# Gated linear attention with a low-rank mixer: turned keys packed in 96 rows, one group's logarithms summed on TensorE, signs from bits, and a rearranged written order

## The chip, the cores and the metric

The kernel runs on one core of a Trainium2 chip. The metric is device time in microseconds, the median of the runs shown. Inputs and outputs are float32 in HBM; the two channel weights and the mixing weights arrive as float64 words and are turned into float32 on the chip.

## The reference

```
B, H, S, D = 4, 8, 768, 48
mag = sqrt(a_re*a_re + a_im*a_im)
scale = minimum(mag, 0.999) / (mag + 1e-06)
a_re_n, a_im_n = a_re*scale, a_im*scale
for t in range(S):
    S_re, S_im = a_re_n*S_re - a_im_n*S_im + outer(k[t], v[t]), a_re_n*S_im + a_im_n*S_re
    y[t] = q[t] @ S_re
x = y with heads side by side            # (4, 768, 384)
u = x + ((x.T @ U) @ V).T                # over the 768 tokens, rank 32
out = u + relu(u @ w_ch1) @ w_ch2        # 384 -> 1536 -> 384
```

The complex gates turn and shrink a 48 x 48 state at each token, in each of 32 heads. The kernel takes the logarithm of the shrinking and the angle of the turning, sums both along the tokens, and works on blocks of 128 tokens with matmuls.

## The kernel before, in words

The tokens of the four sequences form 24 chunks of 128. Two chunks are one group: there are 12 groups, and 12 calls of the mixer, one for each two chunks.

`gates(g)` works on the gates of a group. `magnitudes_of` (line 637) squares the inputs on ScalarE, and takes logarithms and exponentials on ScalarE and VectorE; the log of the gate's size, `l`, is the sum of a limited logarithm and a second logarithm `y` (line 659 for the first group, 663 for the others). For groups 3 and up, `l` is split into two parts of type fp32r. `within` and its `summed` (688) multiply those logs with the constant matrices `mid` and `fore` on TensorE, which sums them along the tokens; ScalarE's exponentials of that are `es` and `ef`, the weights of q and k. `of_blocks` (725) sums them over blocks of tokens, which gives the table `E`, and four DMAs on SyncE's queue copy it to `T`, one for the real, one for the imaginary half, for two sets of heads. `turns_of` (754) takes the arctangent, multiplies it by the sign of `a_re` (array `n`) and makes fractions of a turn of it; `angles` (770) sums those along the tokens on TensorE (`ph`), with an addition of 0.25 a token, and takes the fraction; `waves` makes cosine and sine, `cs`. For groups 0 to 2 (`BITS`) the sign comes from the sign bit, on VectorE (line 678); for the others ScalarE has a Sign pass (682) and an affine pass that divides by pi and adds 0.25 (583).

`prep(i)` (837) works on a chunk: VectorE multiplies q and k by `es`, then by cosine and sine, into `QKC` of 128 x 8 heads x 2 x 64, of which 48 of each 64 columns hold data and the others zeros. TensorE transposes each head's 112 columns (line 860; real part in rows 0 to 47, imaginary part in rows 64 to 111), and ScalarE copies that to `QK` (871). `chain(i)` (882) makes the products of q and k level by level: `inner` (907, 910) and `corners` (971) on TensorE, scalings by `T` on VectorE (387, in `scaled`), copies into `DG` and `AT`, then the state update `dk` (996) and the outputs `y` (1027, 1035). `mixer(m)` (1051) does the mixing and the channel matmuls of two chunks: `up` (1122), `few` (1222, a scheme with fewer products, from mixer 7 on), `down` (1313, 1356). `leave` (1292) writes the output, at the end of the last mixer on SyncE's queue.

The order of the work is written out. Each operation is recorded by `plan.add` with an engine, a planner's cost and a rank; `ORDER` (line 30) gives for each engine, kind and chunk the place of every operation in one order over all engines, 0 to 2670. The kernel emits the operations in that order, so each engine's queue is a subsequence of it, and an engine executes its queue in order. Waits follow from the data. SyncE's queue issues the input loads, the copies of `E` to `T` and of `DG` to `AT`; GpSimd's queue issues the carries of the angle sum from chunk to chunk (line 779) and most outputs.

`SPARE` (line 176) lists places before which TensorE gets filler: `idle(k)` (1507) multiplies the identity with itself into a PSUM tile that is about to be used, k pieces of 128 columns at once and at most `AHEAD` = 3, if such a tile is free:

```
        nc.tensor.matmul(out=to[:, 0:k * 128].rearrange("p (k m) -> p k m", k=k), lhsT=ident,
                         rhs=ident.unsqueeze(1).to_broadcast([128, k, 128]), start=True, stop=True)
```

The functions that the diff touches:

Of the kernel before, what the change touches and what calls it, by code (L numbers as in the profile page):

```python
# [39 lines left out]
        ("POOL", "load"): {0: [14], 1: [34], 1.5: [84], 2: [31]},  # L40
        ("DVE", "load"): {1: [58]},
# [6 lines left out]
        ("ACT", "gates"): {0: [1, 2, 4, 6, 7, 16, 17, 22, 23, 29, 28, 45, 70, 71], 1: [24, 27, 38, 39, 41, 42, 46, 47, 65, 64, 67, 68], 2: [129, 108,  # L48
# [10 lines left out]
        ("DVE", "gates"): {0: [5, 8, 13, 18, 19, 54, 49], 1: [30, 21, 40, 43, 44, 51, 50], 2: [111, 143, 156, 185, 169], 4: [277, 322, 323, 372, 356],  # L59
# [109 lines left out]
        ("POOL", "small"): {0: [932, 933], 1: [1119, 1116, 1117], 2: [1337, 1278, 1338], 3: [1670, 1446, 1515], 4: [1778, 1776, 1777], 5: [2049, 1855,  # L169
        2008], 6: [2154, 2101, 2162], 7: [2343, 2276, 2342], 8: [2633, 2632, 2648], 9: [2629, 2634, 2663], 10: [2635, 2627, 2636]},  # L170
        ("POOL", "angles"): {6: [615], 8: [708, 733], 10: [882, 931], 12: [1097], 14: [1273, 1302], 16: [1472, 1516], 18: [1669], 20: [1879, 1913],
        22: [2039, 2077]},
        ("DVE", "mixing"): {7: [2018, 2019, 2021, 2030, 2032, 2024, 2040, 2102, 2108, 2115, 2120, 2125, 2027]},
}

# [1413 lines left out]
```

## Time and profile before

| | |
|---|---|
| median of 3 runs | 628.38 us (627.25 to 628.86) |
| profiled execution, span | 627.0 us; the page gives the span alone |
| TensorE busy | 609.9 us, 97% |
| VectorE busy | 499.7 us, 80% |
| ScalarE busy | 415.8 us, 66% |
| TensorE line 1122 (`up`) | 116.9 us |
| VectorE line 387 on `QK` | 102.1 us |
| filler, line 1519, up to 160 us | 30.6 us |
| moved over the span | 73 GB/s mean |

How to read it: "busy" is the time in which an engine has at least one instruction at work; matmuls overlap, and a matmul in float32 shows as two rows. PEld is TensorE's weight load. `a<-b` is output and inputs by tile names, then output and input shapes, then `x` and a count; behind the bar stand busy microseconds, mean nanoseconds of one, and the engine's idle time before them with what ended it. In windows, the first number behind the stretch is its length, and PEclk is the granted share of TensorE's clock. In the timeline the first two numbers are the start and the length of a merged piece.

### The profile page before, as it was taken

What the parts mean: (1) busy time and instruction counts of PE and PEld (TensorE: products, weight loads), DVE (VectorE), ACT (ScalarE), POOL (GpSimd) and SP (SyncE); (2) the same over time, 40 slices, a digit from 0 to 9 for tenths busy, and PEclk for the clock granted to TensorE, in tenths of its full rate; (3) what the DMA queues carried; (4) which work ended last, traced back from release to release, by engine and by line L of the source; (5) the groups of instructions that cost most, each with busy time, mean ns of one, the idle gap of its engine ahead of it and who ended that gap; (6) DMA issues with size and microseconds to landing.
All of it is one profiled execution on the core that took longest, in us unless ns stands there. A gap on an engine that the chain in (4) does not pass through costs nothing.

```text
span 627.0 us, 23447 instructions
## 1 busy us (share of the span) xinstructions
PE 609.9 (97%) x10380; PEld 526.2 (84%) x10380; DVE 499.7 (80%) x887; ACT 415.8 (66%) x807; POOL 38.1 (6%) x79
## 2 busy tenths in 40 slices
PE   6998989999999999999999999999999999999998
PEld 3566767666889889889989989888999998999997
DVE  6899999888999979758977867788989884464554
ACT  6999999999898988687787867688433431202010
POOL 5000000000001010010000100000100100000100
PEclk7999999999999999999999999999999999999999
DMA  8864565644143252541512512601203020000101
GB/s 211 191 146 115 135 136 132 155 111 104 33 80 76 50 120 44 99 89 28 99 37 46 113 40 46 124 19 25 63 21 60 9 51 3 1 1 1 45 14 44
DMA packets 173685, 45.74 MB, mean 73 GB/s; under 512 B 167632, under 2 KB 170384, under 8 KB 173584
## 3 DMA queue, kind: packets, MB, share of 16 engines
q1 hardware_dynamic: 171376, 39.90, 30.1%
q0 software_dynamic: 2208, 4.35, 2.1%
q8 instruction: 81, 1.33, 0.9%
q14 instruction: 20, 0.16, 0.1%
HBM read 33.59 MB, written 4.72 MB: 61 GB/s over the span
## 4 chain that ended last, share of the span: by engine, by line
PE 77%; ACT 4%; DVE 3%; DMA 1%; issue 1%; SPq 0%; ACTq 0%; DVEq 0%
PE down L1356 24%; PE up L1122 15%; PE few L1222 11%; PE dk L996 3%; PE tr L860 3%; PE y L1035 3%; PE inner L910 2%; PE down L1313 2%; PE inner L907 2%; PE tot L741 2%; PE y L1027 2%; PE mixed L1089 2%; PE es ps L692 1%; PE ef ps L692 1%; PE uTp L1107 1%; PE corners L971 1%
## 5 line engine op out<-in xcount | busy, mean ns | idle before, releaser
L1122 PE MATMUL up<-uT,w 128*128 128x256 f32 x504 | 116.9, 383 | 0.0
L387 DVE TENSOR_TENSOR QK<-QK,T 112x512 f32<-112x512 f32 (+2 forms) x144 | 102.1, 732 | 8.4 <-PE inner L910 4.3
L1122 PEld LDWEIGHTS up<-uT,w 128*128 128x128 f32 x504 | 93.6, 190 | 12.5
L1356 PE MATMUL down<-w,h 128*128 128x192 f32 x396 | 72.2, 331 | 0.0
L384 ACT ACTIVATE gate<-gate 128x768 f32<-128x768 f32 (+1 forms) x82 | 64.8, 795 | 7.4 <-DVE GS L791 3.2
L1356 PEld LDWEIGHTS down<-w,h 128*128 128x128 f32 x396 | 64.1, 190 | 1.5 <-issue 0.7
L871 ACT COPY QK<-tr 112x512 f32<-112x512 f32 x96 | 51.2, 590 | 14.6 <-PE tr L860 14.3
L390 DVE TENSOR_TENSOR xo<-down,xo 128x192 f32<-128x192 f32 (+1 forms) x79 | 29.9, 387 | 27.5 <-PE down L1356 27.0
L387 DVE TENSOR_TENSOR QKC<-qk,cs 128x768 f32<-128x768 f32 x44 | 41.7, 955 | 6.3 <-ACT cs L384 3.6
L1230 ACT COPY h<-few 128x512 f32<-128x512 f32 x30 | 17.2, 586 | 40.8 <-PE few L1222 40.8
L1356 PE MATMUL down<-stage 128*128 128x192 f32 x198 | 37.6, 331 | 0.0
L1111 ACT COPY uT<-uTp 128x384 f32<-128x384 f32 x22 | 10.0, 479 | 41.4 <-PE uTp L1107 26.9
L1222 PE MATMUL few<-gate,w 128*128 128x128 f32 x280 | 34.8, 275 | 0.0
L1298 POOL DMA_DIRECT2D out_dram<-xo x32 | 19.2, 644 | 243.3 <-DVE xo L390 140.0
L860 PEld LDWEIGHTS tr<-ident,QKC 64*112 64x112 f32 x768 | 24.5, 130 | 10.7 <-issue 4.7
L1222 PEld LDWEIGHTS few<-gate,w 128*128 128x128 f32 x280 | 33.3, 192 | 0.0
L1356 PEld LDWEIGHTS down<-stage 128*128 128x128 f32 x198 | 32.1, 190 | 0.7 <-issue 0.2
L779 POOL DMA_DIRECT2D gate<-F x15 | 12.0, 799 | 327.9 <-DVE w L578 113.5
L860 PE MATMUL tr<-ident,QKC 64*112 64x64 f32 x768 | 29.4, 221 | 2.3 <-DVE QKC L387 1.6
L381 ACT ACT_TABLE_LOAD x24 | 30.8, 1283 | 1.1 <-PEq L1573 0.7
L384 ACT ACTIVATE h<-up 128x512 f32<-128x512 f32 x42 | 24.6, 596 | 9.8 <-PE up L1122 9.5
L976 ACT COPY AT<-corners 32x128 f32<-32x128 f32 x96 | 24.2, 255 | 9.6 <-PE corners L971 8.3
(200 smaller groups left out, 1285.4 us busy)
## 6 DMA issues: line engine op xcount, KB each, us to landing
stage<-in_moe_w_ch_dram SPq DMA_DIRECT2D x12, 768.0 KB, 5.0
qk<-in_q_dram SPq DMA_DIRECT2D x24, 192.0 KB, 3.2
qk<-in_k_dram SPq DMA_DIRECT2D x24, 192.0 KB, 2.7
VP<-in_v_dram SPq DMA_DIRECT2D x24, 192.0 KB, 3.6
gate<-in_a_re_dram SPq DMA_DIRECT2D x22, 192.0 KB, 3.4
gate<-in_a_im_dram SPq DMA_DIRECT2D x22, 192.0 KB, 3.4
AT<-DG SPq DMA_DIRECT2D x96, 32.0 KB, 2.3
T<-E SPq DMA_DIRECT2D x48, 48.0 KB, 2.9
```

The lines of the kernel that those rows point to most:

```text
L381: ACT(1.37, rank, lambda: nc.scalar.preload_act_table_set(name), writes=[TABLE])
L384: return nc.scalar.activation(out=o, in_=i, func=f, **kw)
L387: nc.vector.tensor_tensor(out=o, in0=a, in1=b, op=OP.mult)
L390: nc.vector.tensor_tensor(out=o, in0=a, in1=b, op=OP.add)
L860: nc.tensor.transpose(out=get(*ps[r])[0:DQ, h], in_=get(*qkc)[at, h].rearrange("p u d -> p (u d)")[:, 0:DQ], identity=ident[at, at], tile_ ...
L871: nc.scalar.copy(out=to, in_=a)
L976: ACT(0.36, RR, lambda r=r, u=u: nc.scalar.copy(out=get(*ATi).rearrange("p (a u) t -> p a u t", u=2)[r:r + BLK, :, u, BLK:2 * BLK], in_=ge ...
L996: nc.tensor.matmul(out=get(*dk[r])[x:end, h], lhsT=get(*ks)[at, h, x // DP, 0:end - x], rhs=get(*VPi)[at, h], start=True, stop=True, tile_ ...
L1122: nc.tensor.matmul(out=get(*ps)[:, e], lhsT=w1[:, f, (ff + e) * 128:(ff + e + 1) * 128], rhs=get(*uT)[:, f], start=(f == 0), stop=(f == KD ...
L1222: nc.tensor.matmul(out=get(*ps)[:, q], lhsT=w()[:, q * 128:(q + 1) * 128], rhs=v[0](), start=(n == 0 and q == 0), stop=True, skip_group_ch ...
L1298: queue.dma_start(out=out[b, c * CH:(c + 1) * CH, lo:hi], in_=get("xo", i)[:, lo:hi])
L1356: nc.tensor.matmul(out=get(*to)[:, part], lhsT=x(j), rhs=y[:, j], start=(first and j == 0), stop=(j == KH - 1), skip_group_check=not first)
```

## The change

Four things change. `QKC` is packed: a head has 96 columns, the real and imaginary part side by side, so the transposes, `QK`, `T`, the states and all products over them have 96 rows instead of 112; the state update loads 64 and 48 columns of a head's 96 and the next columns, and 32 columns at the end are zeroed; the memsets of `T` go. In the first group the limited logarithm and `y` are no longer added on VectorE: each sum on TensorE is made of two matmuls into one PSUM tile. The sign comes from the sign bit for every group; ScalarE's Sign and affine pass go, and the 0.25 is added in the pass that splits the angle. And `ORDER` and `SPARE` are replaced: the listing of TensorE has 34 fillers of 83 pieces where it had 46 of 91. In `ORDER`, the lists of every engine differ; the first lines of two are shown. The last output written is a block of 128 x 384 in place of 128 x 192, and on SyncE's queue the second chunk's gate inputs come ahead of the first weight piece.

```diff
-        ("SP", "load"): {0.0: [0, 3, 2666, 2654, 2670], 0.05: [11, 12], 0.1: [9], 1: [10], 1.2: [57], 1.3: [15, 59], 1.4: [83], 2: [35], 2.5: [56,
...
+        ('SP', 'load'): {0.0: [0, 4, 2659, 2642, 2655], 0.05: [6, 14], 0.1: [11], 1: [21], 1.2: [41], 1.3: [44, 59], 1.4: [119], 2: [26], 2.5: [105,
...
-        ("PE", "gates"): {0: [20, 32, 69], 1: [62, 63, 66], 2: [162, 163, 167, 168, 187, 188], 4: [331, 339, 343, 351, 352, 355], 6: [543, 525, 550,
...
+        ('PE', 'gates'): {0: [30, 39, 69], 1: [50, 60, 66], 2: [161, 177, 152, 185, 195, 187], 4: [324, 327, 334, 337, 346, 350], 6: [525, 494, 532,
...
-SPARE = {20: 8, 32: 9, 62: 1, 66: 1, 73: 1, 82: 5, 91: 1, 113: 6, 116: 1, 119: 8, 140: 8, 153: 6, 157: 4, 167: 1, 168: 1, 207: 6, 216: 1, 217: 1, 282:
-         1, 352: 2, 436: 1, 514: 5, 518: 5, 527: 4, 546: 4, 547: 25, 551: 12, 596: 2, 601: 1, 606: 3, 624: 1, 632: 3, 646: 1, 653: 1, 664: 1, 672: 2,
-         678: 5, 694: 1, 695: 1, 717: 1, 718: 2}
+SPARE = {30: 25, 84: 6, 94: 2, 100: 8, 112: 1, 120: 4, 129: 1, 143: 7, 148: 3, 172: 1, 222: 6, 254: 9, 290: 1, 324: 2, 431: 5, 603: 2}
...
+    DQ = 2 * D
     DP = 64
-    DQ = DP + D
...
+    SUMMED = (0,)
...
-    BITS = range(SPLIT[0])
...
-        QKC.append(singles.tile([128, H, 2, DP], FP, name="QKC%d" % n))
-        nc.gpsimd.memset(QKC[n][:, :, :, D:DP], 0.0)
+        QKC.append(singles.tile([128, H * DQ + DP - (DQ - DP)], FP, name="QKC%d" % n))
+        nc.gpsimd.memset(QKC[n][:, H * DQ:], 0.0)
...
-        nc.gpsimd.memset(TS[n], 1.0)
...
-            if on_dve:
+            if g in SUMMED or g in SPREAD:
                 DVE(c_one(W), R1, lambda: nc.vector.tensor_scalar(out=t(l), in0=t(l), scalar1=-0.5, scalar2=-LNMAX, op0=OP.mult,
                                                                   op1=OP.max), [], [L])
-                DVE(cd, R1, lambda: add(t(l), t(l), t(y)), Y, [L])
+                if g not in SUMMED:
+                    DVE(cd, R1, lambda: add(t(l), t(l), t(y)), Y, [L])
...
-            if g in BITS:
-                DVE(c_one(W), R1, lambda: nc.vector.tensor_scalar(out=t(n).bitcast(U32), in0=t(ar).bitcast(U32), scalar1=0x80000000,
-                                                                  scalar2=INV_PI, op0=OP.bitwise_and, op1=OP.bitwise_or), AR, [N])
-            else:
-                ACT(ca + 0.09, R1, lambda: act(t(n), t(ar), AF.Sign, bias=tiny), AR, [N])
+            DVE(c_one(W), R1, lambda: nc.vector.tensor_scalar(out=t(n).bitcast(U32), in0=t(ar).bitcast(U32), scalar1=0x80000000,
+                                                              scalar2=INV_PI, op0=OP.bitwise_and, op1=OP.bitwise_or), AR, [N])
...
-                    PE(0.65, R1, lambda: nc.tensor.matmul(out=get(*to), lhsT=m.bitcast(FP), rhs=of(l, i), start=True, stop=True),
-                       [L, name], [to, ("sums", g, i)], takes=[keeps], steps=2)
+                    def each():
+                        for u, a in enumerate(parts):
+                            nc.tensor.matmul(out=get(*to), lhsT=m.bitcast(FP), rhs=of(a, i), start=(u == 0), stop=(u == len(parts) - 1))
...
-                        out=get(*tt)[u * DP:u * DP + D, 0:hi - lo, w * HH * NTOT:(w + 1) * HH * NTOT],
+                        out=get(*tt)[u * D:(u + 1) * D, 0:hi - lo, w * HH * NTOT:(w + 1) * HH * NTOT],
...
-                        nc.tensor.matmul(out=get(*ps)[u * 64:u * 64 + w, p], lhsT=get(*l)[:, h:h + w], rhs=total, start=True,
-                                         stop=True, tile_position=(0, u * 64))
+                        for n, a in enumerate(parts):
+                            nc.tensor.matmul(out=get(*ps)[u * 64:u * 64 + w, p], lhsT=get(*a)[:, h:h + w], rhs=total, start=(n == 0),
+                                             stop=(n == len(parts) - 1), tile_position=(0, u * 64))
...
-            if g not in BITS:
-                ACT(ca + 0.09, R2, lambda: act(t(z), t(z), AF.Identity, scale=1.0 / math.pi, bias=fourth), [], Z)
...
-                    ACT(c_act(DM), R2, lambda: nc.scalar.copy(out=of(a, i), in_=of(z, i)), [zi], [a + (i,)])
+                    ACT(c_act(DM) + 0.09, R2, lambda: act(of(a, i), of(z, i), AF.Identity, bias=fourth), [zi], [a + (i,)])
...
-                        nc.tensor.transpose(out=get(*ps[r])[0:DQ, h], in_=get(*qkc)[at, h].rearrange("p u d -> p (u d)")[:, 0:DQ],
+                        nc.tensor.transpose(out=get(*ps[r])[0:DQ, h], in_=get(*qkc)[at, h * DQ:(h + 1) * DQ],
...
-                    for x, end in ((0, DP), (DP, DQ)):
-                        nc.tensor.matmul(out=get(*dk[r])[x:end, h], lhsT=get(*ks)[at, h, x // DP, 0:end - x], rhs=get(*VPi)[at, h],
+                    for x, w in ((0, DP), (DP, D)):
+                        nc.tensor.matmul(out=get(*dk[r])[x:x + w, h], lhsT=get(*ks)[at, h * DQ + x:h * DQ + x + w], rhs=get(*VPi)[at, h],
```

More of the change, by code (lines that the diff above doesn't have):

```diff
@@ L30 @@
 ORDER = {
[9 rows of a table removed]
-        ("POOL", "load"): {0: [14], 1: [34], 1.5: [84], 2: [31]},
-        ("DVE", "load"): {1: [58]},
[6 rows of a table removed]
-        ("ACT", "gates"): {0: [1, 2, 4, 6, 7, 16, 17, 22, 23, 29, 28, 45, 70, 71], 1: [24, 27, 38, 39, 41, 42, 46, 47, 65, 64, 67, 68], 2: [129, 108,
[10 rows of a table removed]
-        ("DVE", "gates"): {0: [5, 8, 13, 18, 19, 54, 49], 1: [30, 21, 40, 43, 44, 51, 50], 2: [111, 143, 156, 185, 169], 4: [277, 322, 323, 372, 356],
[10 rows of a table removed]
-        ("ACT", "angles"): {0: [72, 86, 98, 100, 103], 1: [76, 106, 112, 114, 126], 2: [210, 231, 251, 240, 241, 242, 263, 269, 271], 4: [375, 395,
[5 rows of a table removed]
@@ L172 @@
-        22: [2039, 2077]},
-        ("DVE", "mixing"): {7: [2018, 2019, 2021, 2030, 2032, 2024, 2040, 2102, 2108, 2115, 2120, 2125, 2027]},
-}
-SPARE = {20: 8, 32: 9, 62: 1, 66: 1, 73: 1, 82: 5, 91: 1, 113: 6, 116: 1, 119: 8, 140: 8, 153: 6, 157: 4, 167: 1, 168: 1, 207: 6, 216: 1, 217: 1, 282:
-         1, 352: 2, 436: 1, 514: 5, 518: 5, 527: 4, 546: 4, 547: 25, 551: 12, 596: 2, 601: 1, 606: 3, 624: 1, 632: 3, 646: 1, 653: 1, 664: 1, 672: 2,
-         678: 5, 694: 1, 695: 1, 717: 1, 718: 2}
[9 rows of a table added]
+        ('POOL', 'load'): {0: [12], 1: [64], 1.5: [576], 2: [35]},
@@ new lines @@
+        ('DVE', 'load'): {1: [89]},
[6 rows of a table added]
+        ('ACT', 'gates'): {0: [2, 3, 5, 9, 10, 13, 18, 36, 47, 31, 32, 40, 70, 71], 1: [7, 16, 23, 28, 24, 33, 51, 58, 53, 56, 62, 68], 2: [115, 63,
[10 rows of a table added]
+        ('DVE', 'gates'): {0: [8, 1, 19, 15, 48, 54], 1: [17, 20, 34, 29, 72, 61], 2: [92, 140, 151, 196, 158], 4: [247, 314, 316, 342, 330], 6: [432,
[10 rows of a table added]
+        ('ACT', 'angles'): {0: [75, 85, 90, 91, 97], 1: [77, 95, 104, 106, 109], 2: [209, 235, 248, 243, 240, 252, 260, 267, 264], 4: [366, 387, 408,
[5 rows of a table added]
+        ('DVE', 'angles'): {0: [76, 86], 1: [78, 96], 2: [211, 236, 249], 4: [367, 395, 414], 6: [559, 564, 570, 588, 607, 611, 624], 8: [701, 727,
[4 rows of a table added]
@@ new lines @@
+        ('POOL', 'small'): {0: [834, 1095], 1: [1232, 992, 994], 2: [1483, 1384, 1410], 3: [1525, 1450, 1501], 4: [1709, 1777, 1806], 5: [1997, 1963,
+        2007], 6: [2221, 2105, 2227], 7: [2354, 2248, 2340], 8: [2507, 2439, 2536], 9: [2543, 2537, 2538], 10: [2631, 2584, 2649]},
+        ('POOL', 'angles'): {6: [589], 8: [723, 741], 10: [874, 921], 12: [1077], 14: [1241, 1266], 16: [1413, 1472], 18: [1653], 20: [1828, 1874],
+        22: [2002, 2062]},
+        ('DVE', 'mixing'): {7: [1989, 1999, 1991, 2001, 2014, 2009, 2010, 2101, 2108, 2115, 2110, 2114, 2003]},
+}
@@ L695, in summed @@
                 else:
-                    PE(0.65, R1, lambda: nc.tensor.matmul(out=get(*to), lhsT=m.bitcast(FP), rhs=of(l, i), start=True, stop=True),
-                       [L, name], [to, ("sums", g, i)], takes=[keeps], steps=2)
+                    def each():
+                        for u, a in enumerate(parts):
+                            nc.tensor.matmul(out=get(*to), lhsT=m.bitcast(FP), rhs=of(a, i), start=(u == 0), stop=(u == len(parts) - 1))
+                    PE(0.65 * len(parts), R1, each, [L, name] + [y + (i,)] * (g in SUMMED), [to, ("sums", g, i)], takes=[keeps], steps=2 * len(parts))
             psum(ps, "T", [128, DM], [128, 512])
@@ L726, in of_blocks @@
             lo = first
-            ps, e = ("tot", i), ("E", g)
+            ps, e, parts = ("tot", i), ("E", g), (y, l) if g in SUMMED else (l,)
             psum(ps, "T", [128, HH, NTOT])
@@ L744, in of_blocks @@
             else:
-                PE(0.51, R1, sums, [l, ("total", 0), ("sums", g)], [ps], way=1, takes=[e], steps=4 * HH)
+                PE(0.2 + 0.31 * len(parts), R1, sums, [l, ("total", 0), ("sums", g)] + [y + (i,)] * (g in SUMMED), [ps], way=1, takes=[e],
+                   steps=4 * HH * len(parts))
             used = 2 * D if g in SPLIT else 64 + D
@@ L833, in T_of, with turns_of_heads @@
         return get("T", g)[:, i - GROUPS[g][0]].rearrange("p (h b) -> p h b", h=H)[:, :, at:]
+    def turns_of_heads(qkc):
+        return get(*qkc)[:, 0:H * DQ].rearrange("p (h u d) -> p h u d", u=2, d=D)
     def prep(i):
```

39 lines of the change are left out of this document (18 added, 21 removed), and 244 rows, old and new, of the table ORDER.

## The prediction

> **What bounds the kernel now.** The page comes first: TensorE is busy 97% of the span, and only its first slices fall short. VectorE and ScalarE are full there too, and thin out later.
>
> ```profile
> span 627.0 us, 23447 instructions
> ...
> PE 609.9 (97%) x10380; PEld 526.2 (84%) x10380; DVE 499.7 (80%) x887; ACT 415.8 (66%) x807; POOL 38.1 (6%) x79
> ...
> PE   6998989999999999999999999999999999999998
> ...
> DVE  6899999888999979758977867788989884464554
> ACT  6999999999898988687787867688433431202010
> ...
> PEclk7999999999999999999999999999999999999999
> ```
>
> Next, windows by stage: first all work, then (three rows) the filler matmuls of line 1519 alone, which compute nothing that is used. The first number after a window is its length.
>
> ```profile
> core 0: us, PE busy (x) PEld busy (x) DVE busy (x) ACT busy (x) POOL busy (x), PEclk, DMA share, GB/s
> 0.00:30.00 30.00, 23.25 (x118) 13.62 (x118) 23.08 (x50) 22.91 (x45) 8.41 (x32) 0.89 0.84 203
> 30.00:120.00 90.00, 84.07 (x2112) 63.28 (x2110) 88.20 (x140) 86.85 (x169) 0.00 (x0) 1.00 0.58 138
> 120.00:160.00 40.00, 39.00 (x346) 25.11 (x346) 34.76 (x52) 35.56 (x57) 2.50 (x3) 1.00 0.43 100
> 160.00:600.00 440.00, 439.61 (x7644) 400.50 (x7643) 341.28 (x623) 269.34 (x539) 25.01 (x40) 1.00 0.25 51
> 600.00:627.00 27.00, 23.97 (x169) 23.67 (x167) 12.38 (x26) 1.17 (x2) 2.15 (x4) 1.00 0.10 34
> ```
>
> ```profile
> 0.00:30.00 30.00, 14.16 (x36) 8.30 (x36) 0.89 0.84 203
> 30.00:120.00 90.00, 10.43 (x36) 5.80 (x34) 1.00 0.58 138
> 120.00:160.00 40.00, 6.01 (x22) 3.60 (x22) 1.00 0.43 100
> ```
>
> From 160 to 600 us TensorE is idle for 0.4 us in all: there the time is the sum of its own work and nothing else. Everything it loses lies before 160: 6.75 + 5.93 + 1.00 = 13.7 us idle and 30.6 us of filler. In 30:120 VectorE works 88.2 of 90 us and ScalarE 86.9: those two set when TensorE gets work. So the end is TensorE's own work plus what it loses while the other two catch up, plus a tail.
>
> **TensorE's own work.** I gave each TensorE operation the time that it takes between 160 and 600 us (the median step from the end of the one before it, by kind and by what stands before it) and added them in program order: 575.0 us before. The last matmul ends at 622.83 + 1.14 = 623.97 us (tail rows below), so 48.9 us are lost: idle, filler, and the slow clock of the first 30 us (0.89). The same table over the changed program's order gives 575.5.
>
> **What is late, and by how much.** For each TensorE operation I added the VectorE and ScalarE work that stands ahead of it in the written order, each instruction with its own duration less the 0.09 us by which neighbours overlap. Three places of before, in the timeline:
>
> ```profile
> 90.27 0.89 PE L910 MATMUL inner<-QK 112*32 112x48 f32 x64 [0.42 <-DVE QK L387]
> ...
> 142.62 0.92 PE L1089 MATMUL mixed<-r,V 64*128 64x192 f32 x8
> ...
> 156.20 0.89 PE L910 MATMUL inner<-QK 112*32 112x48 f32 x64
> ```
>
> At the first, TensorE has done 52 us of own work and 134 VectorE instructions (81.0 us) stand ahead; it waits for VectorE, 9.3 us behind that sum. At the second, 97 us, 204 instructions, 125.1 us; at the third, 109 us, 222 instructions, 137.7 us. In the changed order the operations with as much own work behind them have 122 (73.2 us), 195 (118.6) and 212 (131.0) ahead: 7.8, 6.5 and 6.7 us less. ScalarE's sums fall by 7.1, 4.9 and 9.6. It isn't so everywhere: at 40 us VectorE has 64.7 instead of 60.6 ahead, at 56 us 80.9 against 81.0 (ScalarE 84.0 against 81.0), at 100 us only 1.8 less (123.9 against 125.6), at 121 us 145.6 against 146.9. What counts is the worst place.
>
> **Step 1, rearranged order and fillers.** Floor of the loss: the tightest distance, 9.3 us, at 58 us of work (ScalarE 84.0) gives 84.0 + 9.3 + 0.7 for the operation itself - 58.5 = 35.5. Ceiling: 48.9, nothing gained. In between, before's own distance at 97 us (142.6 - 125.1 = 17.5) gives 118.6 + 17.5 + 0.9 - 96.6 = 40.4; at 100 us the 1.8 alone gives about 45.7. The later place decides, so I take 44.5: 4.4 less lost. The filler agrees in size: the listing has 83 pieces of 128 columns in 34 matmuls, against 91 in 46, the last at 603 in the written order against 718. Where a filler goes, the work behind it comes sooner only if its operands are there; otherwise it turns into idle time.
>
> **Step 2, the first group's sums.** Groups of rows by form:
>
> ```profile
> L696 PE MATMUL es ps<-GL,mid 128*128 128x384 f32 x8 | 4.2, 606 | 4.1 <-DVE GL L390 3.8 <-ACT es L384 0.3
> L735 PE MATMUL tot<-total,GL 128*64 128x32 f32 x32 | 2.2, 223 | 0.7 <-ACT es L384 0.7
> L390 DVE TENSOR_TENSOR GL<-GL,gate 128x384 f32<-128x384 f32 x2 | 1.1, 568 | 0.3 <-ACT gate L384 0.2
> L578 DVE TENSOR_SCALAR w<-w 128x768 uint32<-128x768 uint32 x12 | 6.7, 562 | 0.0
> L384 ACT ACTIVATE gate<-gate,tiny 128x768 f32<-128x768 f32 x9 | 8.4, 938 | 0.0
> L384 ACT ACTIVATE gate<-gate,fourth 128x768 f32<-128x768 f32 x9 | 8.4, 931 | 2.3 <-DVE gate L760 2.1
> L384 ACT ACTIVATE cs<-F 128x384 f32<-128x384 f32 x44 | 22.4, 518 | 0.2
> L384 ACT ACTIVATE cs<-cs,quarter 128x384 f32<-128x384 f32 x22 | 13.5, 614 | 0.1
> L860 PE MATMUL tr<-ident,QKC 64*112 64x64 f32 x768 | 29.4, 221 | 2.3 <-DVE QKC L387 1.6 <-DVE F L807 0.6
> L860 PEld LDWEIGHTS tr<-ident,QKC 64*112 64x112 f32 x768 | 24.5, 130 | 10.7 <-issue 4.7 <-DVE QKC L387 2.5 <-DVE F L807 1.0
> ```
>
> Two VectorE additions go (2 x 0.57 = 1.1 us, in the sums above). Four matmuls of 384 columns (each fp32 matmul is two rows of the trace) and two sets of block totals are doubled: 4 x 1.05 (4.2 us for the 4 of the first row) + 2 x 0.55 = 5.3 us at the clock of that stretch, in the first 20 us, where filler held most of TensorE. Bounds: 0 (it displaces filler) to 5.3; taken as nothing beyond the 0.5 by which the own work grows, since the order behind it comes out cheaper. If that cover fails, 5.3.
>
> **Step 3, sign from bits.** Nine groups lose a Sign (0.94) and an affine pass (0.93) on ScalarE, 16.8 us; 16 copies gain a bias (0.61 for 0.52), 1.5 us; so 15.3 less. VectorE gains nine of 0.56 = 5.0 us. Most of it lies after 160 us, where VectorE has 99 us free and ScalarE 171: worth 0. The new instruction delays VectorE's queue behind it, the scaling of QK and state updates, by 0.56 each; if every one were met by TensorE, 5.0.
>
> **Step 4, packing in 96.** Instructions on 96 partitions instead of 112 have the same free sizes: 0. The state update still loads 64 and 48 columns. Three memsets of POOL at the start go: POOL then waits for the prefix transfer anyway, 0. The transposes load 96 columns instead of 112; the moving side (64) stays. Bounds 0 and 16/112 of 29.4 = 4.2 us. I take 0: matmuls are busy longer than loads (29.4 to 24.5), which overlap them.
>
> **Step 5, loads and tail.** SP sends the second chunk's gate inputs ahead of prefix and the first weight piece; the first v rows leave behind three of the first totals' transfers instead of ahead of them. Both lie beside a start with filler: 0, or up to the 3.6 us that v takes from issue if the state update met it. At the end:
>
> ```profile
> 622.06 0.56 DVE L390 TENSOR_TENSOR xo<-down,xo 128x384 f32<-128x384 f32 x1 [0.86 <-PE down L1356]
> 622.68 2.04 SPq L1298 DMA_DIRECT2D out_dram<-xo  x2
> 622.83 1.14 PE L1356 MATMUL down<-w,more 128*128 128x192 f32 x6
> 624.01 0.36 DVE L390 TENSOR_TENSOR xo<-down,xo 128x192 f32<-128x192 f32 x1 [1.39 <-PE down L1356]
> ...
> VP<-in_v_dram SPq DMA_DIRECT2D x24, 192.0 KB, 3.6
> gate<-in_a_re_dram SPq DMA_DIRECT2D x22, 192.0 KB, 3.4
> ...
> T<-E SPq DMA_DIRECT2D x48, 48.0 KB, 2.9
> ```
>
> The last addition and output are now a whole row block instead of half: 0.56 - 0.36 = 0.2, and 96 KB more, at 0.5 us for 144 KB between the gate and T rows, 0.3: +0.5.
>
> **Sum.** +0.5 - 4.4 + 0.5 = -3.4: span 627.0 to 623.6. The page gives the execution's span alone; the median of the runs, 628.4, is 1.4 above it, which I carry over: 625.0.
>
> **Rivals.** First, waits take the places of fillers: at 40 and 56 us of work the new order has as much ahead as the old, and if a stall like that, or one inside VectorE's queue, comes later, the loss stays at 48.9 and time is 628.4 + 1.0 = 629.4. For it: VectorE was already 98% busy in 30:120, so a better order has only about 2 us of its idle time to win there. Against it: the smaller sums at 52, 97 and 109 us.
>
> Second, the transposes get cheaper by the whole 4.2 us: 620.8. The busy loads speak for it, their overlap against it. The Trainium skill, TensorE: Matmul & The Clock Gate, LDWEIGHTS, says a weight load's time goes with its columns, at 1.2 per ns; by it each load is 13 ns shorter (an estimate), which shows in the time only if loads bound the transposes. Here a load of 112 columns shows 130 ns, under the matmul's 221.
>
> Third, slower. 25 filler pieces now stand ahead of the first matmul, where 8 stood. TensorE works in order, so the first group waits for all of them:
>
> ```profile
> 1.42 3.58 PE L1519 MATMUL tr<-ident 128*128 128x384 f32 x6 [1.42 <-POOL ident masks.py:199]
> 8.79 1.62 PE L696 MATMUL es ps<-GL,mid 128*128 128x384 f32 x2 [3.79 <-DVE GL L390]
> 10.21 4.05 PE L1519 MATMUL tr<-ident 128*128 128x384 f32 x6
> ...
> 20.33 1.24 PE L1519 MATMUL tr<-ident 128*128 128x384 f32 x4
> ```
>
> The first 8 took 3.58 us, 0.45 each; the 5 at 20.33 took 0.25 each. At 0.45 all 25 end at 1.42 + 11.2 = 12.6 instead of data at 8.8: 3.8 late, and the doubled products at that clock cost 2 x 1.6 more: 625.0 + 7.0 = 632.0. It turns slower by 0.3% once the delay passes 5.3. At 0.25 they end at 7.6 and nothing is lost. The same skill page, Part 1, has half clock as the default and full clock after a busy window of about 3.4 us; by it the pieces would end at 8.5 to 10.2 (an estimate). The slow first fillers and the faster ones at 20.33 agree.
>
> **How the numbers follow.** Forecast 0.50 (own range 622 to 626.4), cheaper transposes 0.11, waits for fillers 0.20, slow fillers 0.19. About 0.3% (1.9 us) is what a measurement tells from no change. Faster: 0.50 + 0.11 = 0.61; same 0.20; slower 0.19. The range reaches to the cheap transposes with some of the floor's gain, 619.0, and just into the slow case, 631.0.
>
> **What would show it.** Filler busy about 25 us, none after 130 us; TensorE idle before 160 us not above 16 us; the first es product at 8.5 to 10.5 and the first ef product right behind it instead of at 14.05; from 160 to 600 again under 1 us idle; ScalarE 15 us less busy, VectorE 4 more; tr matmuls still near 221 ns. Wrong would be: idle grown by what filler lost; waits of TensorE for QK or QKC after 160 us; a first product after 11 us.

## The result, and the profile after

The changed kernel takes 632.61 us (median of 7 runs, 631.98 to 634.36), the kernel before 628.86 (7 runs, 627.25 to 631.07). The ratio is 1.0067, with a 95% interval of 1.0054 to 1.0081: slower by about 4 us, where 625.0 was forecast. The page of the changed kernel:

```profile
span 631.9 us, 23492 instructions
...
PE 613.7 (97%) x10396; PEld 527.5 (83%) x10396; DVE 502.2 (79%) x893; ACT 402.4 (64%) x789; POOL 35.0 (6%) x76
...
PE   9898799999999999999999999999999999999997
...
PEclk9999999899999999999999999999999999999999
...
q8 instruction: 82, 1.34, 0.9%
```

The start is nearly as forecast: TensorE is busy in the first slice, and the clock's row begins with 9 in place of 7 (the first pieces of filler are slow all the same; see the rivals below). ScalarE has 13.4 us less to do, VectorE 2.5 more. New are the 7 in TensorE's fifth slice (63 to 79 us) and the 8 in the eighth slice of the clock (111 to 126 us). The last row is the queue that brings instructions: 1.34 MB in 82 packets, 16 KB each. Windows by stage, first all work (length, then TensorE's busy time), then the filler of line 1520 alone:

```profile
0.00:30.00 30.00, 26.41 (x215) 15.87 (x217) 23.21 (x49) 24.73 (x47) 5.22 (x29) 1.00 0.84 202
30.00:120.00 90.00, 81.47 (x1971) 60.19 (x1965) 83.05 (x136) 82.03 (x159) 0.00 (x0) 0.98 0.53 123
120.00:160.00 40.00, 39.29 (x417) 25.59 (x414) 35.06 (x53) 33.01 (x57) 2.47 (x3) 0.96 0.53 124
160.00:600.00 440.00, 438.13 (x7610) 397.90 (x7609) 347.99 (x633) 259.20 (x523) 26.28 (x42) 1.00 0.26 52
```

```profile
0.00:30.00 30.00, 13.57 (x36) 7.76 (x36) 1.00 0.84 202
30.00:120.00 90.00, 9.85 (x30) 5.03 (x30) 0.98 0.53 123
120.00:160.00 40.00, 0.70 (x2) 0.30 (x2) 0.96 0.53 124
```

Before 160 us TensorE is idle for 3.59 + 8.53 + 0.71 = 12.8 us (13.7 before) and has 24.1 us of filler (30.6 before). So the order delivered what it should: less of both. But from 160 to 600 us it is now idle for 1.9 us instead of 0.4, and the clock is below 1 in two windows. TensorE's waits (sum, times, longest) tell what the idle time waits for:

```profile
PE up L1123 <- issue: 3.1, 1, 3.1
PE dk L997 <- issue: 2.2, 3, 1.3
PE inner L908 <- issue: 1.6, 3, 0.7
```

"issue" means that the engine waited for nothing that the profile shows: no data, no buffer. The waits before had one such row:

```profile
PE inner L907 <- issue: 1.0, 1, 1.0
```

The timeline of the changed kernel shows its longest:

```profile
73.18 1.12 PE L733 MATMUL tot<-total,GL 128*64 128x32 f32 x32
74.23 0.89 PE L911 MATMUL inner<-QK 96*32 96x48 f32 x64
78.20 4.38 PE L1123 MATMUL up<-uT,w 128*128 128x256 f32 x12 [3.08 <-issue]
```

TensorE stands still for 3.08 us, and the 12 matmuls behind take 4.38 us, where 2.86 is their time at full clock (below). Windows around it, and one at 122 us; the number before the last two is PEclk:

```profile
72.66:75.10 2.44, 2.38 (x129) 2.11 (x128) 2.44 (x4) 2.37 (x8) 0.00 (x0) 1.00 0.75 267
75.10:77.90 2.80, 0.02 (x3) 0.00 (x0) 2.60 (x6) 2.76 (x5) 0.00 (x0) 1.00 0.92 184
77.90:81.30 3.40, 3.10 (x7) 2.50 (x8) 3.40 (x6) 3.30 (x6) 0.00 (x0) 0.50 0.85 159
81.30:84.70 3.40, 3.40 (x14) 2.28 (x12) 1.24 (x2) 0.00 (x0) 0.00 (x0) 1.00 0.19 35
122.30:125.70 3.40, 3.40 (x44) 2.42 (x48) 2.94 (x4) 2.21 (x4) 0.96 (x1) 0.50 1.04 261
```

In 2.44 us TensorE goes through 129 + 128 rows, one of them the last of the work before: 256, a packet of 16 KB at 64 bytes each. Then it stops, and for the 3.4 us after the stop the clock is halved. The DMA view between 65.7 and 75.7 us lists no instruction packet; from 75.7 to 78.2 us it lists one:

```profile
q8 instruction: 1, 0.02, 2.4%
```

That packet starts at 75.77, takes 0.98 us, and TensorE goes on at 78.20, 1.45 us after it has landed. I call this a block stop. Counted from the program's start, the rows of TensorE (matmuls, loads, its sequencer's) at which such stops come lie 256 apart: over the traces of both kernels and of the first sixteen experiments, of 57 gaps of 0.4 us or more in both matmuls and loads that end 1.1 to 1.65 us after a packet's end, 52 lie at exactly such a row. The Trainium skill, Runtime: NRT & Kernel Launch, Instruction fetch mechanics, says that instructions come in blocks of 16 KiB, 256 instructions, which agrees with the 82 packets and the distance of the stops. It also says that the fetch hides behind the issue of instructions; here it doesn't, by 3.08 us in one place.

**Account.** To each TensorE operation I gave its median step over the undisturbed stretches of all traces, where the prediction used one stretch of one trace. At the last matmul's end, 623.97 before and 628.44 after (rows below), the difference of 4.5 us is, by this estimate: own work +3.6, block stops +5.2 (1.2 to 6.4), half clock +1.8 (1.4 to 3.2), and filler and waits for data, which are the rest, -6.1. The tail adds 0.5. (The profiled execution of the changed kernel took 633.72, 1.1 above its median, so the spans differ by 4.9 us where the medians differ by 3.8.)

```profile
627.30 1.14 PE L1357 MATMUL down<-w,h 128*128 128x192 f32 x6
...
628.48 0.56 DVE L388 TENSOR_TENSOR xo<-down,xo 128x384 f32<-128x384 f32 x1 [0.35 <-PE down L1357]
```

With operations compared where the same own work is still to come, the changed kernel is ahead between 40 and 50 us, 1 to 3 us behind at 70, some 6.5 behind after the stop at 75, 6 behind at 130 and 1 behind at 160 (estimates, since the orders differ). It falls behind by another 2.5 us between 221 and 252 us, 1.6 of them in three waits for "issue".

### The profile page after: what moved, and what is told of

The parts are those of the page before. It is cut to its first block, busy times and chain, and to the rows that moved or that the text cites. A ratio compares the mean times of both kernels' runs of the same rounds, so it can differ in the third digit from the quotient of the medians.

```text
span 631.9 us, 23492 instructions
## 1 busy us (share of the span) xinstructions
PE 613.7 (97%) x10396; PEld 527.5 (83%) x10396; DVE 502.2 (79%) x893; ACT 402.4 (64%) x789; POOL 35.0 (6%) x76
## 3 DMA queue, kind: packets, MB, share of 16 engines
q8 instruction: 82, 1.34, 0.9%
## 4 chain that ended last, share of the span: by engine, by line
PE 84%; ACT 6%; DVE 5%; issue 2%; DMA 2%; SPq 1%; ACTq 0%; DVEq 0%
PE down L1357 25%; PE up L1123 16%; PE few L1223 11%; PE dk L997 4%; PE y L1036 3%; PE tr L861 3%; PE inner L911 3%; PE down L1314 3%; PE y L1028 2%; PE inner L908 2%; PE tot L739 2%; PE mixed L1090 2%; PE rank L1071 1%; PE uTp L1108 1%; PE ph L794 1%
## 5 line engine op out<-in xcount | busy, mean ns | idle before, releaser
L1123 PE MATMUL up<-uT,w 128*128 128x256 f32 x504 | 118.5, 387 | 3.1 <-issue 3.1
L385 DVE TENSOR_TENSOR QK<-QK,T 96x512 f32<-96x512 f32 (+2 forms) x144 | 102.3, 725 | 4.8 <-PE inner L908 2.5
L872 ACT COPY QK<-tr 96x512 f32<-96x512 f32 x96 | 52.0, 581 | 13.3 <-PE tr L861 13.1
L1223 PE MATMUL few<-gate,w 128*128 128x128 f32 x280 | 36.5, 277 | 0.0
L997 PE MATMUL dk<-VP,QKC 64*64 64x48 f32 (+1 forms) x1408 | 28.1, 217 | 3.8 <-issue 2.2
L861 PEld LDWEIGHTS tr<-ident,QKC 64*96 64x96 f32 x768 | 23.8, 123 | 9.3 <-issue 4.1
L997 PEld LDWEIGHTS dk<-VP,QKC 64*64 64x64 f32 (+1 forms) x1408 | 24.9, 127 | 7.6 <-issue 4.4
```

What stands on the lines that cost most here:

```text
L385: nc.vector.tensor_tensor(out=o, in0=a, in1=b, op=OP.mult)
L861: nc.tensor.transpose(out=get(*ps[r])[0:DQ, h], in_=get(*qkc)[at, h * DQ:(h + 1) * DQ], identity=ident[at, at], tile_position=(r * HC, 0))
L872: nc.scalar.copy(out=to, in_=a)
L997: nc.tensor.matmul(out=get(*dk[r])[x:x + w, h], lhsT=get(*ks)[at, h * DQ + x:h * DQ + x + w], rhs=get(*VPi)[at, h], start=True, stop=True, ...
L1123: nc.tensor.matmul(out=get(*ps)[:, e], lhsT=w1[:, f, (ff + e) * 128:(ff + e + 1) * 128], rhs=get(*uT)[:, f], start=(f == 0), stop=(f == KD ...
L1223: nc.tensor.matmul(out=get(*ps)[:, q], lhsT=w()[:, q * 128:(q + 1) * 128], rhs=v[0](), start=(n == 0 and q == 0), stop=True, skip_group_ch ...
```

## The experiments

The theory is the one just told. The rivals: one of the four parts costs the time by itself; or the searched order is late for data, and the stops only sit where it would wait anyway. Times are medians in us; ratios are to the kernel before on the same chip.

**The parts by themselves.** Kernel before with one part of the change, and with all three:

```diff
 # e7: QKC, QK, T, transposes and state update as in the change (96 rows)
+    DQ = 2 * D
     DP = 64
-    DQ = DP + D
 # e8: signs as in the change; each new VectorE pass half a place behind the Sign that it replaces
+for i in range(6, 24, 2):
+    at = ORDER["ACT", "gates"][i].pop(11 + (i > 6))
+    ORDER["DVE", "gates"][i].append(at + 0.5)
+    ORDER["ACT", "angles"][i].pop(1)
 # e12: the first group's sums as in the change
+for i in (0, 1):
+    ORDER["DVE", "gates"][i].pop(4)
+    SUMMED = (0,)
 # e2: all three
```

> The kernel of before with rows packed in 96 and nothing else. Theory of the prediction: 628.7, within 0.8. Rival (cheaper transposes): 624.5 to 627.

> The kernel of before with the sign from bits in all groups, in the old order, the bit instruction at the place where ScalarE's Sign stood. Theory of the prediction (15 us less ScalarE and 5 us more VectorE lie beside TensorE): 628.7, within 1. Rival one (every delay of VectorE's queue is met by TensorE): up to 633.7. Rival two (ScalarE was on the path after 160 us): 625 to 627.5.

> The kernel of before with the first group's logarithms alone summed on TensorE (36 matmuls more, two VectorE additions fewer). Theory A (3.6 us of own work that nothing hides): 631.5 to 633.5. Theory of the prediction's second step (filler and the wait for VectorE hide it): 628 to 629.5.

> The written order and fillers of before with all three code parts: first group's sums doubled on TensorE, sign from bits everywhere, rows packed in 96. Theory A: 628.9 + 3.7 less what filler would have hidden it = 630.5 to 632.6. Theory B: 628.5 to 629.5, the parts cost nothing. Theory C: anywhere between 627 and 632, and the trace shows whether a wait without a releaser has appeared, since 36 more matmuls stand ahead.

Measured: e7 629.05, 1.0000 [0.9985, 1.0014]; e8 630.05, 1.0021 [1.0008, 1.0035]; e12 631.27, 1.0042 [1.0026, 1.0058]; e2 633.78, 1.0100 [1.0064, 1.0136]. (Where expectations count 36 more matmuls for the sums, it is 20, that is 80 rows: 4 of 384 columns and 16 block totals.) The packing is worth nothing, as forecast. Signs cost 1.3 us, a little more than the theory allowed, and the sums 2.6. All three together (e2) cost 6.3 by the ratio, more than the parts added and more than any theory gave; its runs spread from 632.1 to 640.5, and the excess stays unexplained. In e12 the sums now wait for the logarithms in another place:

```profile
PE es ps L704 <- ACT gate L389: 2.7, 1, 2.7
```

None of these runs has half clock between 15 us and the last matmul, or more than 1.8 us of block stops. So the parts without the order make it slower, and differently from the changed kernel.

**The order by itself, and the change with one part undone.** e1 is the new ORDER and SPARE over the old code of all three parts, that is, the edits of e3, e5 and e6 together:

```diff
 # e3, from the changed kernel: the two additions on VectorE again
+for i, at in ((0, 18.5), (1, 33.5)):
+    ORDER["DVE", "gates"][i].insert(4, at)
-    SUMMED = (0,)
+    SUMMED = ()
 # e5: 112 rows again
-    DQ = 2 * D
     DP = 64
+    DQ = DP + D
 # e6: Sign and affine pass of nine groups on ScalarE again
+    at = ORDER["DVE", "gates"][i].pop()
+    ORDER["ACT", "gates"][i].insert(11 + (i > 6), at + 0.5)
+    ORDER["ACT", "angles"][i].insert(1, ORDER["DVE", "angles"][i][0] + 0.5)
+    BITS = range(SPLIT[0])
```

> The changed kernel's written order and fillers, but the code of before: the first group's logarithms added on VectorE, the sign by ScalarE from the fourth group on, rows packed in 112. Theory A (the first group's doubled sums add about 3.7 us to TensorE's own work, and the rest is unimportant): 632.6 - 3.7 = 628.9 us. Theory B (the written order itself is what costs, by waits): 631.5 to 633. Theory C (TensorE runs out of instructions at places that depend on how many instructions stand ahead): the stall of 3.1 us at 75 us moves or goes, since 36 matmuls fewer stand ahead of it, and the time is 628 to 630, whatever the sums cost.

> The changed kernel with the first group's two logarithms added on VectorE again (two additions of 0.57 us in VectorE's queue, 36 matmuls fewer on TensorE). Theory A: 628.9 to 629.5. Theory B: 632 to 633.5 (VectorE has 1.1 us more). Theory C: 628 to 631 if the stall at 75 us is gone in the trace, 632 if it stands where it stood.

> The changed kernel with rows packed in 112 again (the tile of heads padded to 64, 112 partitions in the transposes, the level products and the read-outs, the three memsets back). Theory of the prediction (partitions carry no time, the transposes are bound by the moving side): 632.6, within 1. Rival (the shorter loads made the transposes cheaper by up to 4.2 us): 634 to 637.

> The changed kernel with Sign and the affine pass on ScalarE again from the fourth group on (15 us more on ScalarE, 5 us less on VectorE), in the changed order. Theory of the prediction (worth nothing, since ScalarE has 171 us free after 160 us): 632.6, within 1.5. Rival (ScalarE's queue is on the path between 160 and 440 us in this order): 640 to 646, with waits of TensorE for ScalarE there; the 12.5 us between the run with all old parts and the run with the sums alone undone would then be this part's.

Measured: e1 643.73, 1.0229 [1.0197, 1.0261]; e3 631.17, 1.0052 [1.0025, 1.0079]; e5 634.04, 1.0075 [1.0060, 1.0089]; e6 643.30, 1.0231 [1.0209, 1.0253]. Undoing the signs alone costs as much as undoing everything, some 10 us more than the changed kernel; none of the three theories for e1 gave that, the rival for e6 did. Up to 120 us e6's trace keeps pace with the changed kernel's. It loses 6.5 us by 160, where 14 us stand at half clock, and 6 more behind 220, 1.9 of them in one wait for ScalarE's copy:

```profile
122.00:136.00 14.00, 13.28 (x89) 6.01 (x82) 6.84 (x11) 7.06 (x13) 0.96 (x1) 0.51 0.71 167
```

```profile
335.01 1.10 PE L872 MATMUL tr<-ident,QKC 64*96 64x64 f32 x31 [1.89 <-ACT QK L883]
```

So the sign bits, which cost 1.3 us in the old order, are what the new order stands on; why the clock stays at half for 14 us without them is not shown. e3 has 80 rows fewer; its stop at 75 us is gone, and others of 1.21 and 1.01 us come at 152 and 197. e5 has the same rows as the changed kernel and the same stop, 3.36 us long. Its 634.04 lies at the edge of what the rival gave, but its trace stays within 1 us of the changed kernel's throughout, and the intervals overlap: the packing has no part in the stop.

**The count of instructions.** Here the filler ahead of the first matmul, 3200 columns in 9 matmuls, is cut into more and narrower ones, so that every later instruction stands further on in its block. In e9 (58 matmuls, 196 rows more):

```diff
+            if at < 40:
+                for w in [64] * 42 + [32] * 16:
+                    idle(max(1, w // 128), min(w, 128), 32)
+                run = 0
+                continue
             idle(min(run, AHEAD))
```

e4 has 50 matmuls of 64 columns (164 rows more), e10 22 (`[384] + [256] + [128] * 20`, 52 more). e14 does the same to the kernel before (its first 17 pieces in 53 matmuls, 188 more).

> The changed kernel with the 25 filler pieces of the start issued as 50 matmuls of half their width in place of 9: the same columns, but 41 matmuls (164 rows of the trace) more stand ahead of all that follows, and nothing else differs. Theory C: the stall of 3.1 us at 75 us moves to another place or goes, together with the half clock behind it; 628.5 to 631. Theories A and B: the stall is not one of instructions, and the time stays at 632.6, within 0.8.

> The changed kernel with the 3200 filler columns of the start cut into 58 matmuls in place of 9, so that 196 more rows of the trace stand ahead of everything else; nothing else differs. Theory C (TensorE's instructions come in blocks of 256 rows, and a block that is used up in less time than the next one takes to come stalls it): laid over the row times of the changed kernel, blocks shifted by 196 rows lose about 2.7 us, against the 6.4 us of such stalls in its own trace: 629 to 631.5 us, no stall over 1 us before 160 us. Rival (the stalls have nothing to do with the count of instructions): 632.6, within 0.8.

> The same with 22 matmuls in place of 9, 52 rows more. Theory C: by the same row times blocks shifted by 52 rows fall worst of all, about 12 us of stalls, the largest near 116, 245, 341, 432 and 509 us: 635 to 640 us. Rival: 632.6, within 0.8.

> The kernel of before with the 17 filler pieces of the start cut into 53 matmuls in place of 6 (188 rows more, the same columns). Theory C: nothing in the old order protects it from stalls at block starts; laid over its own row times the blocks lose 1.3 us as they stand and 12 us shifted by 188 rows. The same reckoning came out too high by half for the run shifted by 52 rows, so 4 to 12 us of stalls in the trace and 631 to 638 us. Rival (the old order is safe wherever its blocks fall, the stalls are a property of the new order): 628.7 to 629.7, stalls under 2 us.

Measured: e9 629.42, 1.0015 [0.9989, 1.0041]; e4 633.07, 1.0071 [1.0043, 1.0100]; e10 631.92, 1.0050 [1.0031, 1.0070]; e14 631.04, 1.0031 [1.0018, 1.0045]. e9's timeline:

```profile
72.78 0.89 PE L911 MATMUL inner<-QK 96*32 96x48 f32 x64
73.59 2.86 PE L1123 MATMUL up<-uT,w 128*128 128x256 f32 x12
```

No stop, and full clock: the same work (the first `es` product starts at 9.48 for 9.27), and 3.2 us less by the count of instructions alone (VectorE is 5.8 us ahead of the changed kernel at 93 us). The packet is no earlier in e9: it starts 3.0 us after TensorE entered the block ahead of it (71.36 to 74.36), as in the changed kernel (72.67 to 75.77, 3.1). But that block lasts e9 until 79.1 us, where it lasted the changed kernel 2.44 us. In e10 the stop splits `inner`, 26 of its 64 matmuls come behind it:

```profile
72.69 0.63 PE L911 MATMUL inner<-QK 96*32 96x48 f32 x38
76.35 0.53 PE L911 MATMUL inner<-QK 96*32 96x48 f32 x26 [3.03 <-issue]
```

Those 26 (with 26 loads) are the 52 rows of shift: the stop moved in the program and stayed at its row. The windows from the start to the stop, of the changed kernel and of e10, count the same 1238 matmul rows and 1238 loads:

```profile
0.00:78.10 78.10, 67.39 (x1238) 43.83 (x1238) 69.41 (x124) 70.55 (x133) 5.22 (x29) 1.00 0.70 162
```

```profile
0.00:76.30 76.30, 67.17 (x1238) 44.97 (x1238) 67.74 (x120) 70.29 (x133) 5.27 (x29) 1.00 0.73 166
```

That settles where the stop comes from. The time was not settled by it: e10's stops still sum to 4.7 us, I had forecast a slower kernel, and its 631.92 is what the rival gave; e4 loses the stop at 75 us but gets one of 1.72 us at 152 and 10.2 us of half clock. And e14 shows that the old order also depends on the count: new stops of 0.78, 0.52 and 0.49 us and +1.8 us in time, the low end of what the theory gave, with under half of its stops. Over the four counts tried the new order's ratios average 1.0051, the old order's two 1.0016: no count here makes the new order the faster one. But stops and time go together: of the kernels with the new order and sign bits for every group, the three whose traces have under 3 us of block stops (e9, e13, e15) have ratios of 1.0011 to 1.0018, the seven with 4 us or more 1.0050 to 1.0094.

**The sums once more, at an equal count.** e13 is e3 with the start filler in 14 matmuls, so that its rows (20 more for the filler, 80 fewer for the sums) stand in their blocks where e9's do:

```diff
-    SUMMED = (0,)
+    SUMMED = ()
+                for w in [384] * 5 + [256] + [128] * 8:
```

> The changed kernel with the first group's logarithms added on VectorE and, for the 80 rows that this takes away, the start's filler cut into 14 matmuls in place of 9 (20 rows more), so that the blocks of 256 rows fall behind the first group as in the run shifted by 196 rows. If stalls at block starts and the doubled sums are the two things that the forecast left out and they add: 629.4 less 1.5 to 2.6 = 627 to 628. If the sums were hidden there: 629.4, within 0.8.

Measured: 630.09, 1.0018 [0.9998, 1.0039], e9's 1.0015 again. TensorE is busy for 5.1 us less than in e9 (608.0 for 613.1), 1.2 of them filler, but idle for 4.6 us more up to the last matmul (15.6 for 11.0). So in the new order the doubled sums cost nothing beside VectorE's additions, as forecast, while the 627 to 628 that I expected here was wrong.

**Filler.** e11 makes the last 23 filler pieces of the kernel before 8 columns wide instead of 128. e15 and e16 put five pieces of filler ahead of the matmul at 122 us, where half clock begins, in e9 and in the changed kernel:

```diff
 # e11
-            idle(min(run, AHEAD))
+            idle(min(run, AHEAD), 8 if at > 600 else 128)
 # e15 (on e9), e16 (on the changed kernel)
-SPARE = {30: 25, 84: 6, 94: 2, 100: 8, 112: 1, 120: 4, 129: 1, 143: 7, 148: 3, 172: 1, 222: 6, 254: 9, 290: 1, 324: 2, 431: 5, 603: 2}
+SPARE = {30: 25, 84: 6, 94: 2, 100: 8, 112: 1, 120: 4, 129: 1, 143: 7, 148: 3, 172: 1, 222: 6, 254: 9, 290: 1, 324: 2, 431: 5, 603: 2, 609: 5}
```

> The kernel of before with its last 23 filler pieces (behind place 600 of the written order, 115 to 150 us) narrowed from 128 to 8 columns, so that the count of instructions stays and 5.4 us of filler time goes. Theory of the prediction's first step (filler that goes lets the work behind it come sooner): 623.5 to 626. Rival one (its place is taken by waits): 628.7, within 0.8. Rival two (without it TensorE falls to half clock there): 629 to 631, with a granted clock under 1 between 115 and 160 us.

> The run shifted by 196 rows with 5 filler pieces more, at place 609 of the written order, where TensorE waits 1.3 us for VectorE (the product called rw ps) and falls to half clock for 3.4 us behind it, so that the product takes 4.5 us in place of 2.8. Theory D (the half clock comes of that idle stretch, which filler covered in the old order): the wait becomes filler, the clock stays at 1.00 between 120 and 130 us, and 629.4 - 1.7 = 627.7. Rival (the time behind it is set by VectorE, so a faster product only waits later): 629.4, within 0.8. Rival two (the filler is in the way): 630 to 630.7.

> The changed kernel with the same 5 filler pieces at place 609 and nothing else. Its half clock at 122 us begins at the read-outs ahead of that product. Theory D: 632.6 - 1.7 = 630.9 if the filler comes in time, and no change (632.6, within 0.8) if the half clock is already decided by the idle gaps ahead of place 609. The stall at 75 us stays in either case.

Measured: e11 628.62, 0.9997 [0.9984, 1.0011]; each narrowed matmul still shows 0.28 to 0.40 us, so only 1.9 us of filler went, and 0.7 came back as idle time between 110 and 160 us. e15 628.70, 1.0011 [0.9992, 1.0029]; e16 632.09, 1.0050 [1.0036, 1.0063]. The spell at 122 us goes in both. The router's product in e9, then in e15:

```profile
121.92 4.46 PE L1146 MATMUL rw ps<-w,rw 128*32 128x512 f32 x24 [1.31 <-DVE rw L1139]
```

```profile
123.88 2.77 PE L1146 MATMUL rw ps<-w,rw 128*32 128x512 f32 x24 [0.38 <-DVE rw L1139]
```

The spell came behind 1.31 us of idle time in e9; with filler there it is gone, and the product 1.7 us shorter. But another spell comes at 106 us in e15, and in e16 the one behind the stop is twice as long: 0.7 and 0.5 us of gain, which the intervals do not tell from none. Idle time is not behind every spell: in the 3.4 us ahead of the one at 106 us no wait is longer than 0.4 us. e15 is the best version of the new order, and no better than the kernel before.

**The transfers ahead of the packet.** e17 moves two loads of 192 KB, issued at 72.35 us in the changed kernel, behind the next two:

```diff
-        413], 9: [409, 372, 373, 377, 382], 9.1: [641], 9.6: [660], 9.7: [460, 618], 10: [638], 10.7: [596, 545], 11: [527, 520, 606, 587, 748], 11.7:
+        413], 9: [409, 383.2, 383.4, 377, 382], 9.1: [641], 9.6: [660], 9.7: [460, 618], 10: [638], 10.7: [596, 545], 11: [527, 520, 606, 587, 748], 11.7:
```

> The changed kernel with two of its loads moved on SyncE's queue: the third group's two loads of a_re (192 KB each, issued at 72.35 us) stand behind its two loads of a_im, some 5 us later; TensorE's instructions and their count stay as they are. Theory: the instruction packet for the stop at 75 us came late because the weight piece (768 KB, issued at 71.12) and these 384 KB stood ahead of it at the DMA engines; with a third of those bytes gone the packet starts by 74.8 instead of 75.77, the stop after 1238 matmul rows falls from 3.08 us to 2.1 or less, and the time to 631 to 632. Rival: the stop hangs on the count of instructions alone: 2.9 to 3.3 us at the same row, time 632.6.

Measured: 634.53, 1.0094 [1.0072, 1.0117], more than either outcome named, and the stop is there, 2.96 us at the same 1238 rows. But the edit did not clear the way: the loads behind moved up, and between 72 and 74 us the DMA engines were still 0.99 busy, now with the 768 KB weight piece:

```profile
72.00:74.00 2.00, 1.70 (x96) 1.52 (x91) 2.00 (x3) 1.92 (x7) 0.00 (x0) 1.00 0.99 361
```

The packet started 3.05 us after TensorE entered its block, as before. Whether transfers make it late stays open; what speaks for it is that over all traces packets start 0.7 us (median) after the block is entered where the DMA engines were under a tenth busy in the 2 us before, and 1.2 where they were over eight tenths, a quarter of those 2.1 or more. The weight piece cannot go earlier, since its buffer comes free only at 71.07 us. Against it speaks e10. There the block was entered at 66.61 us, the engines were quiet up to 69 us, and the packet still started only at 74.09:

```profile
66.60:69.00 2.40, 1.93 (x8) 0.71 (x8) 2.40 (x6) 2.40 (x5) 0.00 (x0) 1.00 0.00 0
```

## Why the prediction was wrong

**The bound, the step that failed.** "So the end is TensorE's own work plus what it loses while the other two catch up, plus a tail", and from 160 to 600 us own work "and nothing else". This left out that TensorE must also be handed its instructions, before 160 us and after. The trace of before had no more than 1.2 us of it to show, 1.0 in one wait for "issue", which I passed over. In the changed kernel block stops take 6.4 us, 3.08 of them at 75 us, and the half clock on top 1.8 more than before. e9 shows it, which takes 3.2 us away by the count alone. How much each stop costs in time is not shown one by one.

**Own work** was forecast at +0.5 and is +3.6 by the table of all traces; without the doubled sums (e3) it is -0.2. The doubled sums are real work of TensorE, so this term of the sum was too small by 3.1.

**Step 1, order and filler.** The mechanism was right: filler fell by 6.5 us over the windows, and filler and waits for data by 6.1 in the account, against a forecast of 4.4. What the step lacked is what else the order sets: which instructions share a block. 32 `corners`, 32 block totals and 64 `inner` of 10 to 40 ns each now follow each other amid transfers of 267 GB/s, and use up a block in 2.44 us. And in every run of the new order some half clock begins between 76 and 123 us; in none of the old one does any begin between 15 us and the last matmul.

**Step 2, the sums: 0.** Held in the new order (e13 beside e9), where 3.6 us of own work displace filler and waits. It would not have held in the old one: +2.6 (e12), half of the ceiling of 5.3.

**Step 3, sign bits: 0.** As a part for itself it is +1.3 (e8). But the sum had no term for what it is to the order: undone in the new order it costs 10 us (e6), half of it between 120 and 160 us and half behind 220, where the forecast counted on ScalarE's free time. The order was laid out for a ScalarE without those passes.

**Step 4, packing: 0.** Right (e7, e5). The transposes' row in the changed kernel, this shape alone:

```profile
L861 PE MATMUL tr<-ident,QKC 64*96 64x64 f32 x768 | 28.7, 220 | 1.2 <-DVE QKC L385 1.2
```

220 ns for 221, while the load fell from 130 to 123 ns. The second rival is out.

**Step 5, tail: +0.5.** Right: 631.9 - 628.44 = 3.5 us behind the last matmul, 3.0 before. The 1.4 us carried over from span to median is 1.8 in the profiled execution (633.72 - 631.9), 0.4 more.

**The rivals.** The third, slow filler at the start, came only in part:

```profile
1.42 8.01 PE L1520 MATMUL tr<-ident 128*128 128x384 f32 x18 [1.42 <-POOL ident masks.py:199]
9.27 0.81 PE L693 MATMUL es ps<-gate,mid 128*128 128x384 f32 x2
...
10.56 0.81 PE L693 MATMUL ef ps<-gate,fore 128*128 128x384 f32 x2
```

25 pieces took 8.01 us, 0.32 each; the first product came at 9.27, inside the 8.5 to 10.5 forecast, and `ef` close behind. The filler's rows from 1.4 to 6.0 us, then from 6.7 to 9.0:

```profile
L1520 PE MATMUL tr<-ident 128*128 128x384 f32 x7 | 4.8, 870 | 1.4 <-POOL ident masks.py:199 1.4
```

```profile
L1520 PE MATMUL tr<-ident 128*128 128x384 f32 x8 | 2.7, 486 | 0.0
```

Up to 6.1 us these rows start 0.64 us apart, as in the half clock of before, and behind it 0.32. The windows show a clock of 1.00 for both, but the trace has no clock record before 6.2 us. So the slow filler was there and ended in time. The slow first products of before belong to its order: e7 and e11 begin with the same work, and though their windows show 1.00 (their records begin at 14.4 us or are missing), their first `es` product takes 1.62 us, where the changed kernel's takes 0.81:

```profile
8.70 1.62 PE L699 MATMUL es ps<-GL,mid 128*128 128x384 f32 x2 [3.50 <-DVE GL L391]
```

The first rival, waits in the place of filler, is nearest in its sense, since idle time comes back after a good start, but not in its mechanism: the waits for data fell. The slower outcome came by a way that no rival named; that the third rival's 632.0 is near 632.61 is luck.

**What stays open.** The best count and filler (e15, 628.70) is still 3.7 us above the forecast. Its remaining block stops are 2.6 us and its half clock about 1.7; beyond the size of these two I have no experiment that takes them away.

## What to carry to other kernels

In a kernel of many short matmuls, read the waits for "issue". Where 256 instructions of TensorE are used up within a few microseconds, as in 2.44 us here, look for a stop: some such blocks had one of 0.4 to 3.4 us behind them, many had none, and half clock came behind the longest of them, but not behind every one of 1 to 2 us. Compare two versions at the same count of instructions, or at several, before laying a difference of under 1% on the edit itself. And an order that was searched for a set of parts is one with them: its parts can't be priced one by one in the old order.

## What the runs showed of the hardware that was not expected

- In these traces no packet of 256 instructions starts before TensorE is within 41 rows of the block ahead of it; TensorE stops when it has used that block up, and goes on 1.22 to 1.58 us (median 1.37) after the packet has landed. Most packets take 0.9 to 1.5 us, and none follows another by less than 3.2 us.
- Half clock comes in spells of 3.41 us or multiples of it, such as those behind 3.08 us of idle time at 75 us and 1.31 at 122 us (e9). The Trainium skill, TensorE: Matmul & The Clock Gate, Part 1, has windows of about 3.4 us for the clock; the lengths agree.
- A filler matmul of 8 columns instead of 128 still shows 0.28 to 0.39 us on TensorE (e11).
- A granted clock of 1.00 in the windows can also mean that the trace has no record there: at the start of the changed kernel matmuls of 384 columns start 0.64 us apart under it, and 0.32 apart from 6.1 us on.
